# A retention and gated-FFN kernel: q of the first 512 tokens in 1-KB pieces, and tables made by one multiply each

## The chip, the cores and the metric

The kernel runs on one core of a Trainium2 chip. The metric is the device time of one execution in microseconds (us). A core has a matmul engine (TensorE, "PE" in the profile, with its weight loads as "PEld"), VectorE ("DVE"), ScalarE ("ACT"), GpSimd ("POOL"), SyncE ("SP", which here issues transfers), and 16 DMA engines that move data between HBM and the on-chip memory SBUF. PE writes its results to PSUM, eight banks of 2 KB a partition; PE, DVE and ACT are ordered among each other by semaphores, and each works through its own instructions in order.

## The reference

```python
# q, k, v: (8, 8, 576, 64) float32; x: (4608, 512); w_gate, w_val: (512, 1536); w_out: (1536, 512)
scores = scale * np.matmul(q, k.transpose(0, 1, 3, 2))
gamma = 1.0 - 2.0 ** (-5.0 - np.arange(H, dtype=np.float32))
rel = pos[:, None] - pos[None, :]
Dmat = np.where(rel >= 0, gamma[:, None, None] ** rel[None, :, :], 0.0)
ret = scores * Dmat[None, :, :, :]
attn = np.matmul(ret, v)
x = attn.transpose(0, 2, 1, 3).reshape(B * S, H * D)
gate = 1.0 / (1.0 + np.exp(-(x @ w_gate)))
out = (gate * (x @ w_val)) @ w_out
```

Eight batches of eight heads go through a causal attention without softmax whose scores decay by a factor per head and distance; its output, 4,608 tokens by 512, goes through a gated feed-forward layer.

## The kernel before

The decay gamma^(i-j) is split: q is multiplied by gamma^i (and the scale), k by gamma^-j, from small tables, while both are cast from float32 to bf16. What remains of the decay is the causal mask, multiplied into the scores on their way out of PSUM. Tokens are worked in chunks of 128; what earlier chunks contribute comes through a state (k transposed times v, summed over tokens, `st`), so that a chunk needs only its own scores (`intra`) and one product of q with the state before it (`inter`).

The first 768 tokens are worked as three pairs of chunks, `PAIRS`: pair 0 and pair 1 are tokens 0 to 255 and 256 to 511 of batch 0, pair 2 is the first 256 tokens of batch 1. The rest runs later, in steps of one chunk, beside the feed-forward matmuls of finished tokens.

A pair A is loaded by `load_pair` in six transfers of 256 KB on SP: k, q, k, q, v, v, each of four heads (half g = 0 or 1), two neighbouring tokens a partition, so that a contiguous piece is 2 tokens x 64 x 4 B = 512 B. Pairs 0 and 1 are issued first: k and q of both halves of pair 0, then of pair 1, then the four transfers of v, then the weights of the feed-forward layer. All of them use one pool of 18 buffers, `ld`.

Each half is then worked as follows. `cast_pair` multiplies by the table and casts (k on POOL, q on DVE; v is cast alone, on POOL). `turn` calls `pair_t`: four PE transposes of 128 x 128 put two heads by 64 dimensions on the partitions, into one PSUM bank, and ACT copies that bank to SBUF. k keeps its two token parities apart (`kT`), while q is written into token order (`qT`), that is to every second element. `pair_qk` makes the scores of a half in 16 small matmuls into two banks, and DVE multiplies them by the mask `trip` into `ptp`. Then follow `pair_intra`, `pair_st` (the state matmuls), `tile_sv` (ACT copies the state to `sbd`), `pair_inter` and `pair_out` (a copy to `xT`, the input of the feed-forward layer).

The order of the instructions of each engine is written out by hand: the statements at the end of the function give it, one after the other, and each engine takes its own in that order. The groups of matmuls called `fill(n)`, 4n of them on a blank tile into a bank that nobody reads, stand between the first steps. The turned k of a half goes through the bank of pool `tr` and the turned q through that of `pv` (one buffer each); the last q turn uses a bank of pool `ffn`. `pv` and `tr` later hold the outputs of pair 0.

The tables are made by `tables`: an iota of token positions on POOL, for each head one multiply by log(gamma) on DVE, and an exponential each for k and q on ACT. It is called for the pairs (positions 2p + r in each of two 256-token blocks) and for the single chunks.

The start of the order, as written:

```python
    cast_pair("q", 0, 0, nc.vector)
    turn("k", 0, 0, *TR)
    turn("q", 0, 0, *PV)
    fill(3)
    cast_pair("q", 0, 1, nc.vector)
    pair_qk(0, 0, QK)
    turn("k", 0, 1, *TR)
    fill(2)
    turn("q", 0, 1, *PV)
    fill(3)
```

Of the kernel before, what the change touches and what calls it, by code (L numbers as in the profile page):

```python
# [9 lines left out]
FP32 = mybir.dt.float32  # L10
BF16 = mybir.dt.bfloat16
AF = mybir.ActivationFunctionType
ALU = mybir.AluOpType
# [3 lines left out]
def kernel(  # L17
# [30 lines left out]
    consts = ctx.enter_context(tc.tile_pool(name="consts", bufs=1))  # L48
    ld_pool = ctx.enter_context(tc.tile_pool(name="ld", bufs=18))
# [4 lines left out]
    osb_pool = ctx.enter_context(tc.tile_pool(name="osb", bufs=13))  # L54
# [12 lines left out]
    PAIRS = [(0, 0), (0, 1), (1, 0)]  # L67
# [28 lines left out]
    parts = {}  # L96
# [9 lines left out]
            tiles.append(t)  # L106
        loaded[s] = tiles

    def load_pair(A):

        b, a2 = PAIRS[A]
        for nm, src, g in (("k", k, 0), ("q", q, 0), ("k", k, 1), ("q", q, 1), ("v", v, 0), ("v", v, 1)):
            t = ld_pool.tile([P, M, 2, D], FP32, tag="ld", name=f"{nm}32p_{A}_{g}")
            nc.sync.dma_start(  # L114
                out=t.rearrange("p h r d -> p h (r d)"),
                in_=src[b, g * M:(g + 1) * M, a2 * 2 * P:(a2 + 1) * 2 * P, :].rearrange("h (p r) d -> p h (r d)", r=2))
            parts[nm, "pair", A, g] = t
            yield

    def load_w(f, nf):  # L120

        for nm, src in (("g", moe_w_gate), ("v", moe_w_val)):
            for i in range(nf):
                r = NKC // nf
                t = ld_pool.tile([P, r, nf * P], FP32, tag="ld", name=f"w{nm}32_{f}_{i}")
                nc.sync.dma_start(
                    out=t, in_=src[i * r * P:(i + 1) * r * P, f * P:(f + nf) * P].rearrange("(c p) f -> p c f", p=P))
                parts[nm, f, i] = t

    def load_wo(f):  # L130
        t = ld_pool.tile([P, DM], FP32, tag="ld", name=f"wo32_{f}")
        nc.sync.dma_start(out=t, in_=moe_w_out[f * P:(f + 1) * P, :])
        parts["o", f] = t

    both = [load_pair(A) for A in range(2)]
    for n_pair in (4, 2):
        for one in both:
            for _ in range(n_pair):
                next(one)
    load_w(0, 2)  # L140
    load_w(2, 2)
    load_w(4, 4)
    load_w(8, 4)
    pair_2 = load_pair(2)
    for n_wo, n_pair in ((2, 4), (6, 2), (4, 0)):
        for _ in range(n_wo):
            load_wo(sum(1 for x in parts if x[0] == "o"))
        for _ in range(n_pair):
            next(pair_2)
    LEAD_CAST = 3  # L150


# [5 lines left out]
    def idle_bank():  # L158
        idle.append(ffn_psum.tile([P, P], FP32, tag="ffn", name=f"idle_{len(idle)}"))
# [9 lines left out]
    def tables(shape, pattern, step, put):  # L169

        pos = consts.tile([P, pattern[0][1], pattern[1][1]], FP32, name=f"pos{step}")
        nc.gpsimd.iota(pos, pattern=pattern, base=0, channel_multiplier=step,
                       allow_small_or_imprecise_dtypes=True)
        arg = consts.tile(shape, FP32, name=f"arg{step}")
        qt = consts.tile(shape, FP32, name=f"qtab{step}")
        kt = consts.tile(shape, FP32, name=f"ktab{step}")
        for h in range(H):
            nc.vector.tensor_scalar_mul(put(arg, h), pos, math.log(1.0 - 2.0 ** (-5.0 - h)))
        nc.scalar.activation(out=kt, in_=arg, func=AF.Exp, bias=0.0, scale=-1.0)
        nc.scalar.activation(out=qt, in_=arg, func=AF.Exp, bias=lnscale, scale=1.0)  # L180
        return qt, kt

    lnscale = consts.tile([P, 1], FP32)
    nc.vector.memset(lnscale, math.log(1.0 / math.sqrt(D)))
    qtab2, ktab2 = tables([P, 2, H, 2], [[2 * P, 2], [1, 2]], 2, lambda t, h: t[:, :, h, :])
    ident = consts.tile([P, P], BF16)
    make_identity(nc, ident)
    qtab, ktab = tables([P, NC, H, 1], [[P, NC], [1, 1]], 1, lambda t, h: t[:, :, h, :])
# [46 lines left out]
    natural = {}  # L235
    turned = {}

    def cast_pair(nm, A, g, eng):

        if (nm, A) not in natural:  # L240
            natural[nm, A] = osb_pool.tile([P, 2, H, D], BF16, tag="osb", name=f"{nm}p_{A}")
        o = natural[nm, A][:, :, g * M:(g + 1) * M, :].rearrange("p r h d -> p h r d")
        i = parts.pop((nm, "pair", A, g))
        if nm == "v":
            eng(out=o, in_=i)
        else:
            tab = (ktab2 if nm == "k" else qtab2)[:, PAIRS[A][1], g * M:(g + 1) * M, :].unsqueeze(3).to_broadcast([P, M, 2, D])
            eng.tensor_tensor(out=o, in0=i, in1=tab, op=ALU.mult)

    def cast_k(s):  # L250

        b, c = STEPS[s]
        n = width[c]
        k32 = loaded[s][0]
        kn = qk_nat[s % NB][:, 1:3]
        for j in range(n // 64):
            for hh in range(2):
                nc.gpsimd.tensor_tensor(  # L258
                    out=kn[half(hh), j, :, half(hh)], in0=k32[half(j), hh::2, :],
                    in1=ktab[half(j), c, hh::2].unsqueeze(2).to_broadcast([64, M, D]), op=ALU.mult)  # L260
        natural["k", s] = kn
# [38 lines left out]
    turned = {}  # L300
# [6 lines left out]
    def half(x):  # L307
        return slice(x * 64, x * 64 + 64)
# [3 lines left out]
    def pair_t(nm, A, g, psum, tag, eng):  # L312
        ps = psum.tile([P, 2, 2, P], BF16, tag=tag, name=f"{nm}Tp_{A}_{g}")
        for i in range(2):
            for r in range(2):
                m = 2 * g + i
                nc.tensor.matmul(ps[:, i, r, :], lhsT=natural[nm, A][:, r, 2 * m:2 * m + 2, :], rhs=ident,
                                 is_transpose=True, start=(i == 0 and r == 0), stop=(i == 1 and r == 1))
        if nm == "k":
            if g == 0:  # L320
                turned["kp", A] = osb_pool.tile([P, M, 2, P], BF16, tag="osb", name=f"kT_{A}")
            o = turned["kp", A][:, 2 * g:2 * g + 2]
        else:
# [3 lines left out]
        eng(out=o, in_=ps)  # L327
# [45 lines left out]
    def pair_intra(A, g, a):  # L373
        s = 2 * A + a
        if s not in pair_ps:
            pair_tile(A, a, [(tr_psum, "tr") if a else (pv_psum, "pv")])
        for i in range(2):
            m = 2 * g + i
            ps, at_m, of = pair_ps[s][m]
            for r in range(2):  # L380
                for hh in range(2):
                    nc.tensor.matmul(ps[half(hh), at_m, :], lhsT=natural["v", A][half(a), r, 2 * m + hh, :],
                                     rhs=probs["p", A][half(a), hh, m, r, :],
                                     start=(at_m == 0 and r == 0), stop=(at_m == of - 1 and r == 1),
                                     skip_group_check=True)
# [224 lines left out]
    def turn(nm, A, g, pool=ffn_psum, tag="ffn"):  # L610
        pair_t(nm, A, g, pool, tag, on_act)
# [23 lines left out]
    for A in range(2):  # L635
        for g in range(2):
            cast_pair("k", A, g, nc.gpsimd)
# [7 lines left out]
    QK = [(qk_psum, "qk"), (qk_psum, "qk")]  # L645
    FF = [(ffn_psum, "ffn"), (ffn_psum, "ffn")]
    TR, PV = (tr_psum, "tr"), (pv_psum, "pv")
    cast_pair("q", 0, 0, nc.vector)
    turn("k", 0, 0, *TR)
    turn("q", 0, 0, *PV)  # L650
    fill(3)
    cast_pair("q", 0, 1, nc.vector)
    pair_qk(0, 0, QK)
    turn("k", 0, 1, *TR)
    fill(2)
    turn("q", 0, 1, *PV)
# [12 lines left out]
    fill(3)  # L669
    pair_intra(0, 0, 0)  # L670
    pair_qk(1, 1, FF)
    pair_intra(0, 0, 1)
# [205 lines left out]
```

## Time and profile before

| | before |
|---|---|
| median of 9 runs | 335.19 us (335.04 to 335.61) |
| the profiled execution, whole | 335.19 us |
| its span in the profile | 333.5 us |
| weight loads of PE (PEld) busy | 190.3 us, 57% |
| HBM read, written | 37.75 MB, 9.44 MB |
| packets of the main DMA queue | 163,920 |

The span runs from the first to the last profiled instruction; some 1.7 us of the whole time lie around it. Busy times overlap between engines. In a row of the timeline the first number is the start in us from the span's start, the second the length, then come engine, line, operation, what is written from what, and in square brackets how long the engine had been idle before and what ended that idle time. L248 is the cast of q or k in `cast_pair`, L327 the copy in `pair_t`, L336 the scores, L341 the mask, L382 `pair_intra`, L351 `pair_st`, L362 `tile_sv`, L400 `pair_out`, L245 the cast of v. A matmul's shape is given as rows x columns of its weights and then of what streams through.

The loads of the first pairs, in the page's part on DMA issues (KB each, median us from issue to landing):

```profile
k32p<-in_k_dram SPq DMA_DIRECT2D x6, 256.0 KB, 5.0
q32p<-in_q_dram SPq DMA_DIRECT2D x6, 256.0 KB, 5.2
v32p<-in_v_dram SPq DMA_DIRECT2D x6, 256.0 KB, 6.0
```

### The profile page before, as it was taken

The numbers are of one execution on the slowest core, as the hardware profiler recorded it, in microseconds if no ns is written. First come the engines' busy times: TensorE is split into PE (matmuls) and PEld (weight loads), VectorE is DVE, ScalarE is ACT, GpSimd is POOL, SyncE is SP. The second block draws the span as 40 slices with busy tenths as digits, with TensorE's granted clock in tenths as the row PEclk, the third lists the DMA queues.
The fourth block names the chain that finished last, engine by engine and source line by source line (L and its number), as shares of the span: only waits on it lengthen the run. The fifth ranks groups of instructions, "written<-read, shape, count | busy, mean of one in ns | idle before, by whom it ended". The sixth has DMA issues, their size and how long they took to land.

```text
span 333.5 us, 7568 instructions
## 1 busy us (share of the span) xinstructions
PE 326.9 (98%) x2868; PEld 190.3 (57%) x2868; DVE 168.5 (51%) x337; ACT 167.5 (50%) x345; POOL 183.5 (55%) x322
## 2 busy tenths in 40 slices
PE   8899999999999999999999999999999999999996
PEld 7764546869566566566566555544555455444443
DVE  6847749726476166345247636442674256504320
ACT  6554636547466365355456554445546455233321
POOL 5588558788979977572458966572677400000000
PEclk9999999999999999999999999999999999999999
DMA  8999999999999999999756999599765950020002
GB/s 222 316 373 361 322 243 174 203 183 210 191 232 185 191 225 187 275 198 248 146 104 139 203 222 192 115 209 264 136 129 81 272 188 0 2 95 31 2 31 94
DMA packets 164100, 60.00 MB, mean 180 GB/s; under 512 B 144480, under 2 KB 156000, under 8 KB 164064
## 3 DMA queue, kind: packets, MB, share of 16 engines
q1 hardware_dynamic: 163920, 59.39, 84.6%
q8 instruction: 22, 0.36, 0.5%
q10 hardware_dynamic: 144, 0.13, 0.1%
q14 instruction: 14, 0.11, 0.1%
HBM read 37.75 MB, written 9.44 MB: 141 GB/s over the span
## 4 chain that ended last, share of the span: by engine, by line
PE 89%; DMA 4%; DVE 2%; SPq 2%; issue 1%; ACT 1%; POOL 0%; DVEq 0%
PE h L506 49%; PE op L572 24%; PE hg L621 3%; PE hv L621 3%; DMA q<-in_q_dram 2%; PE pv L431 2%; PE qk L410 2%; DMA v32p<-in_v_dram 2%; PE pv L429 2%; PE st L443 2%; SPq L114 2%; PE op L562 1%; DVE vbd L279 1%; PE hg L700 1%; PE hv L700 1%
## 5 line engine op out<-in xcount | busy, mean ns | idle before, releaser
L506 PE MATMUL h<-xT,wg_sb 128*128 128x384 bf16 (+2 forms) x480 | 102.8, 337 | 0.3 <-DVE gv L534 0.2
L506 PE MATMUL h<-xT,wv_sb 128*128 128x384 bf16 (+2 forms) x480 | 102.8, 337 | 0.0
L258 POOL TENSOR_TENSOR qk_nat<-k,ktab 64x256 bf16<-64x256 f32 x120 | 73.8, 615 | 43.2 <-PE st L443 30.2
L534 DVE TENSOR_TENSOR gv<-g,h 128x384 bf16<-128x384 bf16 (+1 forms) x96 | 59.7, 621 | 71.8 <-PE h L506 56.3
L572 PE MATMUL op<-wo_sb,gv 128*128 128x512 bf16 x372 | 85.5, 379 | 0.0
L530 ACT ACTIVATE g<-h 128x384 bf16<-128x384 f32 (+1 forms) x96 | 52.2, 544 | 64.9 <-PE h L506 58.3
L449 DVE CAST sbd<-st 64x256 bf16<-64x256 f32 x104 | 43.7, 420 | 45.1 <-PE st L443 42.9
L506 PEld LDWEIGHTS <-wg_sb 128*128 128x128 bf16 x480 | 43.6, 98 | 31.8 <-DVE ob L549 0.6
L506 PEld LDWEIGHTS <-wv_sb 128*128 128x128 bf16 x480 | 44.1, 98 | 29.0 <-issue 0.4
L279 POOL CAST vbd<-v 64x256 bf16<-64x256 f32 x116 | 46.4, 400 | 16.4 <-PE pv L431 11.9
L572 PEld LDWEIGHTS <-gv 128*128 128x128 bf16 x372 | 34.3, 98 | 36.3
L289 ACT CAST vs<-v 64x256 bf16<-64x256 f32 x104 | 41.9, 403 | 2.4 <-DMA v<-in_v_dram 0.8
L549 ACT COPY ob<-op 128x512 f32<-128x512 f32 x33 | 19.3, 586 | 46.2 <-PE op L572 44.9
L268 POOL TENSOR_TENSOR qk_nat<-q,qtab 128x512 bf16<-128x512 f32 (+1 forms) x32 | 33.3, 1042 | 2.6 <-POOL qk_nat L258 0.2
L433 ACT CAST xT<-pv 128x512 bf16<-128x512 f32 (+1 forms) x34 | 18.2, 534 | 18.1 <-PE pv L431 18.0
L412 DVE TENSOR_TENSOR pt<-qk,tri 128x512 bf16<-128x512 f32 (+1 forms) x34 | 21.2, 625 | 6.1 <-PE qk L410 5.8
L443 PEld LDWEIGHTS <-qk_nat 128*128 128x128 bf16 x208 | 13.2, 98 | 8.7
L431 PE MATMUL pv<-pt,vbd 128*128 128x64 bf16 x240 | 18.0, 193 | 0.0
L431 PEld LDWEIGHTS <-vbd 128*128 128x128 bf16 x240 | 15.2, 98 | 3.5
L429 PE MATMUL pv<-T,sbd 128*128 128x64 bf16 x216 | 17.2, 193 | 0.0
L429 PEld LDWEIGHTS <-sbd 128*128 128x128 bf16 x216 | 15.1, 98 | 2.5
L522 DVE TENSOR_TENSOR gv<-g,h 128x256 bf16<-128x256 bf16 x24 | 10.0, 420 | 11.9 <-ACT g L520 11.4
(84 smaller groups left out, 242.8 us busy)
## 6 DMA issues: line engine op xcount, KB each, us to landing
out_dram<-ob SPq DMA_DIRECT2D x34, 256.0 KB, 2.9
k<-in_k_dram SPq DMA_DIRECT2D x26, 256.0 KB, 3.9
q<-in_q_dram SPq DMA_DIRECT2D x26, 256.0 KB, 4.6
v<-in_v_dram SPq DMA_DIRECT2D x26, 256.0 KB, 5.3
wg<-in_moe_w_gate_dram SPq DMA_DIRECT2D x12, 256.0 KB, 6.1
wv<-in_moe_w_val_dram SPq DMA_DIRECT2D x12, 256.0 KB, 5.4
wo<-in_moe_w_out_dram SPq DMA_DIRECT2D x12, 256.0 KB, 5.3
k32p<-in_k_dram SPq DMA_DIRECT2D x6, 256.0 KB, 5.0
```

Source lines behind the costliest of these rows:

```text
L258: nc.gpsimd.tensor_tensor(out=kn[half(hh), j, :, half(hh)], in0=k32[half(j), hh::2, :], in1=ktab[half(j), c, hh::2].unsqueeze(2).to_broadc ...
L268: eng.tensor_tensor(out=qs[0:n], in0=q32[0:n], in1=qtab[0:n, c, :].unsqueeze(2).to_broadcast([n, H, D]), op=ALU.mult)
L279: eng(out=vb[half(hh), j, :, half(hh)], in_=v32[half(j), hh::2, :])
L289: nc.scalar.copy(out=natural["vs", s][half(hh), j], in_=loaded[s][2][half(j), hh::2, :])
L412: nc.vector.tensor_tensor(out=pt[:, :, 0:n].rearrange("p m (j t) -> p m j t", t=64), in0=qkp[:, :, 0:n].rearrange("p m (j t) -> p m j t", ...
L429: nc.tensor.matmul(pvp[:, m, half(j)], lhsT=before[:, m, :], rhs=qT[:, m, half(j)], start=True, stop=False)
L431: nc.tensor.matmul(pvp[:, m, half(j)], lhsT=vb[:, j, m, :], rhs=pt[:, m, half(j)], start=before is None, stop=True)
L449: nc.vector.tensor_copy(out=sb[half(hh), :, half(hh)], in_=st_tiles[b][half(hh)])
L506: nc.tensor.matmul(out, lhsT=w_sb[:, kc, fc * P:(fc + 1) * P], rhs=xT[:, kc, t0 + a:t0 + e], start=(kc == 0), stop=(kc == NKC - 1))
L530: nc.scalar.activation(out=g[:, 0:n], in_=h1[:, 0:n], func=AF.Sigmoid)
L534: nc.vector.tensor_tensor(out=gvs[some[0]][:, a:e], in0=g[:, 0:n], in1=h2[:, 0:n], op=ALU.mult)
L572: nc.tensor.matmul(opp, lhsT=gvs[fc][:, nb * P:(nb + 1) * P], rhs=wo_sb[:, fc, :], start=(fc == 0), stop=(fc == NFC - 1))
```

## The change

q of pairs 0 and 1 (tokens 0 to 511 of batch 0) is no longer loaded by pair. Four transfers `load_quads(m)` of the same 256 KB each take two heads and all 512 tokens, four neighbouring tokens a partition, so that a contiguous piece is 1 KB. Partition p then holds tokens 4p to 4p + 3, so partitions 0 to 63 belong to pair 0 and 64 to 127 to pair 1. `cast_quads` multiplies and casts one such tile on DVE with a table of its own (`qtab4`); `turn_quads` transposes it in four PE instructions; two tiles (four heads, m even and odd) share the PSUM bank of pool `pv`; and `take_quads(A, g)` copies on ACT the columns of one pair out of that bank into `qT`, to every fourth element. There are as many casts, transposes and copies of q as before, but each copy takes half of the columns of two transposed tiles, and the bank is free only when both pairs' copies are done.

The order of the loads becomes k, q, q, k, q, q, then k twice, then v; the order of the first steps is rewritten, with 15 groups of fillers after the first ten instead of 14, all casts of q ahead of the first mask on DVE, and no second idle bank. k, v and the whole of pair 2 are loaded and worked as before.

The tables are made with one multiply by a tile of eight log(gamma) values, set by eight memsets, in place of eight multiplies by a constant; a third call makes `qtab4`.

```diff
-    both = [load_pair(A) for A in range(2)]
-    for n_pair in (4, 2):
-        for one in both:
-            for _ in range(n_pair):
-                next(one)
+    def load_quads(m):
+
+        t = ld_pool.tile([P, 2, 4, D], FP32, tag="ld", name=f"q32q_{m}")
+        nc.sync.dma_start(out=t.rearrange("p h r d -> p h (r d)"),
+                          in_=q[0, 2 * m:2 * m + 2, 0:4 * P, :].rearrange("h (p r) d -> p h (r d)", r=4))
+        parts["q", "quads", m] = t
+
+    for g in range(2):
+        load_part("k", 0, g)
+        for i in range(2):
+            load_quads(2 * g + i)
+    for g in range(2):
+        load_part("k", 1, g)
+    for A in range(2):
+        for g in range(2):
+            load_part("v", A, g)
...
-        for h in range(H):
-            nc.vector.tensor_scalar_mul(put(arg, h), pos, math.log(1.0 - 2.0 ** (-5.0 - h)))
...
+    decay = consts.tile([P, H], FP32)
+    for h in range(H):
+        nc.vector.memset(decay[:, h:h + 1], math.log(1.0 - 2.0 ** (-5.0 - h)))
...
+        nc.vector.tensor_tensor(out=arg, in0=pos.unsqueeze(2).to_broadcast([P, n, H, r]),
+                                in1=decay.unsqueeze(1).unsqueeze(3).to_broadcast([P, n, H, r]), op=ALU.mult)
...
+    ktab2, qtab2 = tables(2, 2, 2 * P, 2, "kq")
+    qtab4, = tables(1, 4, 0, 4, "q")
...
+    def cast_quads(m):
+        if m % 2 == 0:
+            natural["quads", m // 2] = osb_pool.tile([P, 2, 4, 2, D], BF16, tag="osb", name=f"qq_{m // 2}")
+        o = natural["quads", m // 2][:, m % 2].rearrange("p r h d -> p h r d")
+        tab = qtab4[:, 0, 2 * m:2 * m + 2, :].unsqueeze(3).to_broadcast([P, 2, 4, D])
+        nc.vector.tensor_tensor(out=o, in0=parts.pop(("q", "quads", m)), in1=tab, op=ALU.mult)
+
+    quads = {}
+
+    def turn_quads(m, psum, tag):
+        if m % 2 == 0:
+            quads[m // 2] = psum.tile([P, 2, 4, P], BF16, tag=tag, name=f"qTq_{m // 2}")
+        for r in range(4):
+            nc.tensor.matmul(quads[m // 2][:, m % 2, r, :], lhsT=natural["quads", m // 2][:, m % 2, r, :, :], rhs=ident,
+                             is_transpose=True, start=(m % 2 == 0 and r == 0), stop=(m % 2 == 1 and r == 3))
+
+    def take_quads(A, g):
+        if ("qp", A) not in turned:
+            turned["qp", A] = osb_pool.tile([P, M, 2 * P], BF16, tag="osb", name=f"qT_{A}")
+        nc.scalar.copy(out=turned["qp", A][:, 2 * g:2 * g + 2, :].rearrange("p m (t r) -> p m r t", r=4),
+                       in_=quads[g][:, :, :, half(A)])
...
-    cast_pair("q", 0, 0, nc.vector)
+    for m in range(2):
+        cast_quads(m)
     turn("k", 0, 0, *TR)
-    turn("q", 0, 0, *PV)
+    turn_quads(0, *PV)
+    fill(2)
+    turn_quads(1, *PV)
+    take_quads(0, 0)
     fill(3)
-    cast_pair("q", 0, 1, nc.vector)
+    for m in range(2, 4):
+        cast_quads(m)
     pair_qk(0, 0, QK)
     turn("k", 0, 1, *TR)
+    take_quads(1, 0)
     fill(2)
-    turn("q", 0, 1, *PV)
+    turn_quads(2, *PV)
+    turn_quads(3, *PV)
+    take_quads(0, 1)
     fill(3)
-    cast_pair("q", 1, 0, nc.vector)
+    turn("k", 1, 0, *TR)
     pair_qk(0, 1, FF)
-    turn("k", 1, 0, *TR)
-    turn("q", 1, 0, *PV)
-    fill(2)
-    cast_pair("q", 1, 1, nc.vector)
+    take_quads(1, 1)
+    fill(3)
     turn("k", 1, 1, *TR)
     pair_qk(1, 0, QK)
-    fill(1)
-    turn("q", 1, 1)
-    idle_bank()
-    fill(3)
+    fill(2)
     pair_intra(0, 0, 0)
     pair_qk(1, 1, FF)
```

More of the change, by code (lines that the diff above doesn't have):

```diff
@@ L107, in load @@
         loaded[s] = tiles
[L109 to L118, printed above, removed]
     def load_w(f, nf):
@@ L133, in load_wo, with load_part @@
         parts["o", f] = t
-    both = [load_pair(A) for A in range(2)]
-    for n_pair in (4, 2):
-        for one in both:
-            for _ in range(n_pair):
-                next(one)
+    def load_part(nm, A, g):
+        b, a2 = PAIRS[A]
+        t = ld_pool.tile([P, M, 2, D], FP32, tag="ld", name=f"{nm}32p_{A}_{g}")
+        nc.sync.dma_start(
+            out=t.rearrange("p h r d -> p h (r d)"),
+            in_={"k": k, "q": q, "v": v}[nm][b, g * M:(g + 1) * M, a2 * 2 * P:(a2 + 1) * 2 * P, :].rearrange(
+                "h (p r) d -> p h (r d)", r=2))
+        parts[nm, "pair", A, g] = t
+    def load_quads(m):
[12 more added lines that the diff above has]
+            load_part("v", A, g)
     load_w(0, 2)
@@ L143 @@
     load_w(8, 4)
-    pair_2 = load_pair(2)
+    pair_2 = iter((("k", 0), ("q", 0), ("k", 1), ("q", 1), ("v", 0), ("v", 1)))
     for n_wo, n_pair in ((2, 4), (6, 2), (4, 0)):
@@ L148 @@
         for _ in range(n_pair):
-            next(pair_2)
+            nm, g = next(pair_2)
+            load_part(nm, 2, g)
     LEAD_CAST = 3
@@ L168, with tables @@
     fill(10)
[L169 to L176, printed above, removed]
-        for h in range(H):
-            nc.vector.tensor_scalar_mul(put(arg, h), pos, math.log(1.0 - 2.0 ** (-5.0 - h)))
-        nc.scalar.activation(out=kt, in_=arg, func=AF.Exp, bias=0.0, scale=-1.0)
-        nc.scalar.activation(out=qt, in_=arg, func=AF.Exp, bias=lnscale, scale=1.0)
-        return qt, kt
     lnscale = consts.tile([P, 1], FP32)
     nc.vector.memset(lnscale, math.log(1.0 / math.sqrt(D)))
-    qtab2, ktab2 = tables([P, 2, H, 2], [[2 * P, 2], [1, 2]], 2, lambda t, h: t[:, :, h, :])
+    decay = consts.tile([P, H], FP32)
+    for h in range(H):
+        nc.vector.memset(decay[:, h:h + 1], math.log(1.0 - 2.0 ** (-5.0 - h)))
+    def tables(n, r, base, step, which):
+        pos = consts.tile([P, n, r], FP32, name=f"pos{step}")
+        nc.gpsimd.iota(pos, pattern=[[base, n], [1, r]], base=0, channel_multiplier=step,
+                       allow_small_or_imprecise_dtypes=True)
+        arg = consts.tile([P, n, H, r], FP32, name=f"arg{step}")
+        nc.vector.tensor_tensor(out=arg, in0=pos.unsqueeze(2).to_broadcast([P, n, H, r]),
+                                in1=decay.unsqueeze(1).unsqueeze(3).to_broadcast([P, n, H, r]), op=ALU.mult)
+        made = []
+        for nm in which:
+            t = consts.tile([P, n, H, r], FP32, name=f"{nm}tab{step}")
+            if nm == "k":
+                nc.scalar.activation(out=t, in_=arg, func=AF.Exp, bias=0.0, scale=-1.0)
+            else:
+                nc.scalar.activation(out=t, in_=arg, func=AF.Exp, bias=lnscale, scale=1.0)
+            made.append(t)
+        return made
+    ktab2, qtab2 = tables(2, 2, 2 * P, 2, "kq")
+    qtab4, = tables(1, 4, 0, 4, "q")
     ident = consts.tile([P, P], BF16)
     make_identity(nc, ident)
-    qtab, ktab = tables([P, NC, H, 1], [[P, NC], [1, 1]], 1, lambda t, h: t[:, :, h, :])
+    ktab, qtab = tables(NC, 1, P, 1, "kq")
     qtab = qtab.rearrange("p c h o -> p c (h o)")
```

## The prediction

> **What bounds the kernel now.** I read the page first (shares, chain of waits), then the chain in order of time up to 45 us, then the timeline of the first 20 us with the windows of that stretch, and last the timeline around 50 us.
>
> The page's busy shares, one row of five engines:
>
> ```profile
> PE 326.9 (98%) x2868; PEld 190.3 (57%) x2868; DVE 168.5 (51%) x337; ACT 167.5 (50%) x345; POOL 183.5 (55%) x322
> ```
>
> TensorE (PE) is busy nearly the whole span of 333.5 us; what an edit at the start can win or lose is how early PE's dense stream begins. The chain in order of time (start, length, what) says what set that:
>
> ```profile
> 6.52 6.47 DMA v32p<-in_v_dram
> 12.99 0.05 issue
> 13.04 0.63 POOL vp L245
> 13.67 0.04 issue
> 13.71 0.39 PE st L351 x12
> ```
>
> The start is bound by the tenth load, the second half of v of pair 0: it lands at 12.99, GpSimd (POOL) casts it, and PE's state matmuls (`pair_st(0, 0)`) end at 14.10. From there the chain is PE and the short ACT copies of the state. So transfers set the start, and q's four of 256 KB each lie before v in the queue. The windows (width, PE, PEld, DVE, ACT, POOL, granted clock, DMA share, GB/s) show the queue saturated, at two rates:
>
> ```profile
> 11.00:12.00 1.00, 1.00 (x30) 0.91 (x29) 0.83 (x2) 0.61 (x2) 0.61 (x1) 1.00 1.20 294
> 15.00:16.00 1.00, 1.00 (x42) 0.86 (x43) 0.39 (x2) 0.60 (x2) 0.85 (x2) 1.00 1.09 348
> ```
>
> At 11 us the pieces are 512 B (q, k, v of a pair); at 15 us mostly the first weights, in 1-KB pieces. 256 KB take 262/294 = 0.89 us in the first and 262/348 = 0.75 us in the second.
>
> How close behind the transfers the engines are is seen in the timeline of the first 15 us:
>
> ```profile
> 4.58 0.81 DVE L248 TENSOR_TENSOR qp<-q32p,qtab 128x512 bf16<-128x512 f32 x1 [0.55 <-DMA q32p<-in_q_dram]
> 5.88 0.73 ACT L327 COPY qT<-qTp 128x512 bf16<-128x512 bf16 x1
> 6.67 0.42 PE L336 MATMUL qkp<-qT,kT 64*64 64x128 bf16 x16 [0.15 <-ACT qT L327]
> 8.91 0.42 PE L336 MATMUL qkp<-qT,kT 64*64 64x128 bf16 x16 [0.15 <-ACT qT L327]
> 12.54 0.41 PE L382 MATMUL pvp<-ptp,vp 64*64 64x128 bf16 x8
> 13.71 0.38 PE L351 MATMUL st<-vp,kp 64*64 64x64 bf16 x12 [0.30 <-POOL vp L245]
> 14.92 0.44 PE L351 MATMUL st<-vp,kp 64*64 64x64 bf16 x16 [0.58 <-ACT sbd L362]
> ```
>
> PE waited only 0.30 us for the cast of v. That is the whole slack between the q/k path and the transfers: if the path becomes later by more than about half a microsecond, it sets the start in v's place.
>
> Far later one more place matters: near 50 us VectorE (DVE) waits a little for a transfer before a chain of DVE work that holds PE up:
>
> ```profile
> 49.29 1.09 DVE L268 TENSOR_TENSOR qk_nat<-q,qtab 128x512 bf16<-128x512 f32 x1 [0.17 <-DMA q<-in_q_dram]
> ...
> 53.83 0.61 PE L506 MATMUL h<-xT,wg_sb 128*128 128x256 bf16 x4
> ```
>
> **What the Trainium skill says.** "DMA: Bandwidth & Descriptors", section "Why small descriptors are slow (HBM only)", gives each packet a fixed overhead of about 3 cycles beside one cycle for 32 B: 19 cycles for 512 B, 35 for 1 KB, so 1 KB should be 8% faster. The trace agrees in sign and shows more, 348 against 294 GB/s (18%). "SBUF — State Buffer", section "Door 1: The DMA port swizzle (why `[64,N]` ≈ `[32,N]`)", speaks of 16-byte lines and says that two-byte elements may be strided up to 8 apart for free. The trace differs: ScalarE (ACT) pays for a stride of 2:
>
> ```profile
> L327 ACT COPY kT<-kTp x6: 580/586/586, 5.3 to 39.5; 128x512 bf16<-128x512 bf16 x6
> L327 ACT COPY qT<-qTp x6: 735/739/742, 5.9 to 40.2; 128x512 bf16<-128x512 bf16 x6
> ```
>
> Same size, contiguous 586 ns, every second element 739 ns. The new copy writes every fourth element; no row shows one.
>
> **The change part by part.**
>
> Tables: 16 multiplies of about 0.1 us (1.59 us together) become 8 memsets and 3 multiplies, one ACT row more (about 0.14 us at ACT's spacing) and one iota more on POOL (about 0.2 us). The first cast of k waits for its transfer until 3.80 with POOL idle 0.85 us before it, ACT is free until 5.34, DVE waits for q until 4.58 with 0.55 idle. All hidden, value 0. Without that cover it would be 0.2 us late on POOL.
>
> Transfers: same 256 KB each, same number, on SP before the same things. The four q transfers go from 0.89 to 0.75 us: v lands 4 x 0.14 = 0.56 us earlier, at about 12.4, and its cast ends at 13.1. Bounds: 0.3 us (the page's 8%) to 0.6. This would be the gain if v still ended last.
>
> Order: q of pairs 0 and 1 is now held in tiles of two heads by 512 tokens. The first score block of pair 0 needs two such tiles (second and third transfer) instead of one. Step by step, with PE at about 0.055 us a filler or turn (the timeline has 12 fillers in 0.83 and four turns in 0.40: 0.43 for eight more, so 0.23 for four and 0.17 to drain), 0.35 for 16 score matmuls (6.67 to the next start at 7.02), hand-over 0.05:
> - tile 0: cast on DVE 4.43 to 5.2 (4.58 less 0.15); tile 1: the third landing was 1.33 after the second (POOL starts 5.91 against 4.58), less 0.14: cast 5.6 to 6.3. Four turns on PE 6.35 to 6.6, drained 6.77. ACT copy 6.8 to 7.55. Scores (0,0) at 7.6, before 6.67: 0.9 late.
> - turn of k (0,1) at 7.95 (its cast ends near 7.5). ACT: k copy 8.4 to 9.0, then q's copy for pair 1 to 9.65. Tiles 2 and 3 are turned into the same PSUM bank, so they wait for that copy: PE 9.7 to 10.15, with fill(2) before it and about 1 us idle. Queued behind are the turns and scores of everything later. ACT copies to 11.1; scores (0,1) at 11.15, before 8.91: 2.2 late.
> - From there the new order is shorter: two q turns and their waits before scores (1,0) are gone. fill(3), turn of k (1,1), scores (1,0) at 12.45 (before 10.97), fill(2), `pair_intra(0,0,0)` at 13.25 (before 12.54), scores (1,1), `pair_intra(0,0,1)`, state matmuls from 14.1 to 14.6 (before 14.10). Late by 0.5.
> - DVE: its q casts are all before the first mask, so masks run 8.75 to 10.0, 11.7 to 13.0, 13.0 to 14.3 and 14.3 to 15.6 (four pairs of 1.29; before the last ended at 14.51). The copy of the first output tile then ends at 16.3 instead of 15.11, and frees the bank for `pair_intra(1,0,0)`: PE there at 16.35 instead of 15.62. Late by 0.7. Unknown: 0.5 if DVE catches up.
>
> Fillers: 24 groups of four become 25, 0.23 us; contained in the steps above. The second idle bank goes; no instruction.
>
> Later: weights land 0.56 earlier, and the casts of them are not what PE waits for there. From 17 to 48 us PE is dense, so the shift is carried. At 49.29 the 0.17 us wait for q's transfer takes up that much of it. Loads of pair 2 and the later steps are unchanged.
>
> Sum: 0.7 - 0.17 = about +0.5 us. The profiled execution is 335.19 us, 1.7 over its span, and equals the median: forecast 335.7. Own range 335.3 to 336.1: the third landing 0.4 earlier takes 0.4 off until k's cast binds, three ACT copies in series on the path at +0.1 each add 0.3.
>
> **Rivals.**
> - Faster: v keeps ending last. Then the whole 0.56 arrives: 334.6. For it: slack existed, the tail of the old q turns disappears, and one late transfer less would pull the first steps in. Against: two transfers before the first scores and the shared bank. Needs the path to be 0.8 us quicker than my steps.
> - Slower: ACT's stride-4 copy. Place: three of the four copies (first of tile pair 0, pair 1's from the same bank, first of tile pair 1) are in series with PE. Price: stride 2 cost 0.153 us over contiguous; if stride 4 costs two to three times that, 0.89 to 1.05 us each, the path is 0.45 to 0.9 us later, 336.2 to 336.6; taken at 0.95: 335.7 + 3 x 0.21 = 336.3. It decides from about 0.80 us a copy on (3 x 0.06 brings 335.86).
> - No difference: the 0.5 is absorbed by the ACT and DVE waits after 14 us (0.58 us in the row at 14.92) and at 50 us: 335.2. Against: those waits are on state copies that move along with PE.
>
> **How the numbers follow.** A measurement of this kernel can tell 0.2%, 0.67 us: faster is below 334.52, slower above 335.86. Chances: forecast 0.44, slow copies 0.31, v still last 0.16, absorbed 0.09. Slower: all of the slow copies and 0.4 of the forecast's, 0.31 + 0.18 = 0.49. Faster: three quarters of v still last, 0.12. Same: 0.39. The range 334.6 to 336.7 leaves out half of the fast case (0.08) and the top of the slow one (0.1).
>
> **What would show it.** Right: scores (0,0) near 7.6 and (0,1) near 11.2; a PE gap of about 1 us before the turns of tiles 2 and 3 ended by ACT; v's cast near 12.5 with nobody waiting for it; state matmuls ending at 14.4 to 14.8; ACT copies of q near 0.74 us. Wrong: PE again waiting for v's cast (the fast case), copies over 0.8 us (the slow one), q transfers still 0.89 us apart (the pieces bring nothing), or a PE shift at 20 us that is gone by 60 us for another reason.

## The result and the profile after

| | before | after |
|---|---|---|
| median | 335.22 us, 31 runs (334.49 to 338.15) | 337.68 us, 10 runs (336.98 to 338.30) |
| ratio, 95% interval | | 1.0068 (1.0052 to 1.0085) |
| profiled execution, its span | 335.19, 333.5 us | 336.98, 335.3 us |

The change costs about 2.3 us by the ratio (0.68% of 335.2); forecast were +0.5 us and a range up to 336.7. Some executions of most versions run with a lowered clock for a few microseconds near the start and take 1 to 4 us more; they are in the medians and in the ratios alike, and "at full clock" below means a median without them (for after 337.31, 2.1 us above before).

TensorE's busy time, in the page's busy shares, did not change (326.9 us before), nor did the share:

```profile
PE 327.0 (98%) x2872; PEld 191.3 (57%) x2872; DVE 169.2 (50%) x332; ACT 169.6 (51%) x346; POOL 184.8 (55%) x323
```

So the 1.8 us by which the span grew are time in which PE stood still, at the start. The timeline of after (start, length, engine, line, what; in brackets the idle time before and what ended it) shows where. L275 is the cast of q, L283 its transposes, L289 the copy of q on ACT, L378 the scores, L424 `pair_intra`, L442 the copy `xT`:

```profile
6.11 0.69 DVE L275 TENSOR_TENSOR qq<-q32q,qtab 128x512 bf16<-128x512 f32 x1 [0.67 <-DMA q32q<-in_q_dram]
...
7.30 1.30 ACT L289 COPY qT<-qTq 128x512 bf16<-128x512 bf16 x1 [0.75 <-PE qTq L283]
8.65 0.42 PE L378 MATMUL qkp<-qT,kT 64*64 64x128 bf16 x16 [0.72 <-ACT qT L289]
9.91 1.30 ACT L289 COPY qT<-qTq 128x512 bf16<-128x512 bf16 x1
11.27 0.61 PE L283 MATMUL qTq<-ident,qq 128*128 128x128 bf16 x8 [1.43 <-ACT qT L289]
11.91 1.31 ACT L289 COPY qT<-qTq 128x512 bf16<-128x512 bf16 x1 [0.69 <-PE qTq L283]
13.27 0.42 PE L378 MATMUL qkp<-qT,kT 64*64 64x128 bf16 x16 [0.50 <-ACT qT L289]
...
17.48 1.28 DVE L442 CAST xT<-pvp 128x512 bf16<-128x512 f32 x2
18.21 0.63 PE L424 MATMUL pvp<-ptp,vp 64*64 64x128 bf16 x24 [0.19 <-POOL wv_sb L245]
```

Three times in this stretch PE stands still until a copy of q ends on ACT, and each copy takes 1.30 us, not the 0.74 of before. All four are alike, as the view of the tile `qT` says (min, median and max in ns):

```profile
L289 ACT COPY qT<-qTq x4: 1300/1304/1309, 7.3 to 13.5; 128x512 bf16<-128x512 bf16 x4
```

v is no longer waited for by PE. In the timeline of POOL its first two casts run one after the other without a wait, and those that wait now serve steps that are not due yet:

```profile
11.71 1.29 POOL L265 CAST vp<-v32p 128x512 bf16<-128x512 f32 x2
13.27 0.62 POOL L265 CAST vp<-v32p 128x512 bf16<-128x512 f32 x1 [0.28 <-DMA v32p<-in_v_dram]
```

The second half of v of pair 0 landed at 12.33, before at 12.99, close to the 12.4 of the forecast, but this is in part luck. The first half landed at 11.46, before at 11.22: up to there nothing was gained, since the third transfer landed 1.67 us behind the second, before 1.36. Then before had a pause: its second half of v came 1.77 us behind the first, where 0.9 is usual. In after a pause (1.31) falls two transfers later. Past both pauses 0.25 us are left, as the cast of the last half of v shows, which waits for its transfer in both (after, then before):

```profile
14.58 0.62 POOL L265 CAST vp<-v32p 128x512 bf16<-128x512 f32 x1 [0.69 <-DMA v32p<-in_v_dram]
```

```profile
14.83 0.62 POOL L245 CAST vp<-v32p 128x512 bf16<-128x512 f32 x1 [0.25 <-DMA v32p<-in_v_dram]
```

The place of such pauses changes from one execution to another: in e11 below, which is the kernel before once more, the fourth transfer comes 1.94 us behind the third. Their cause is not known. What was gained nobody could use.

The chain of waits, which went through v's load before, now leaves the transfers of q, k and v out:

```profile
11.47 6.08 DMA wv<-in_moe_w_val_dram
17.55 0.05 issue
17.61 0.63 POOL wv_sb L245
18.23 0.61 PE pvp L424 x23
```

This is to be read with care. `pair_intra` does not use the weights; it needs the PSUM bank that the copy `xT` frees. The first of the two copies in the row at 17.48 takes 0.68 us and ends at 18.16, some 0.06 us before POOL's cast, so the chain took the one that came last; PE begins at 18.21. In two other versions with the same order (e3 and e5 below) the same row names DVE's copy.

Later, part of the delay is made up. The first `h` matmul of the stretch near 50 us is 1.79 us late (55.62 against 53.83), the first `hg` was 2.47 late (19.70 against 17.23). DVE's wait of 0.17 us for a transfer of q is gone from its row:

```profile
51.10 0.67 DVE L310 TENSOR_TENSOR qk_nat<-q,qtab 128x512 bf16<-128x512 f32 x1
...
55.62 0.60 PE L548 MATMUL h<-xT,wg_sb 128*128 128x256 bf16 x4
```

From there to the end the distance stays at 1.8 us.

### The profile page after: what moved, and what is told of

It reads as the page before. It is cut to its first block, busy times and chain, and to the rows that moved or that the text cites. A ratio compares the mean times of both kernels' runs of the same rounds, so it can differ in the third digit from the quotient of the medians.

```text
span 335.3 us, 7576 instructions
## 1 busy us (share of the span) xinstructions
PE 327.0 (98%) x2872; PEld 191.3 (57%) x2872; DVE 169.2 (50%) x332; ACT 169.6 (51%) x346; POOL 184.8 (55%) x323
## 4 chain that ended last, share of the span: by engine, by line
PE 92%; SPq 3%; DMA 2%; issue 1%; DVE 1%; ACT 0%; POOL 0%
PE h L548 49%; PE op L614 24%; PE op L837 3%; PE hv L663 3%; PE hg L663 3%; PE pv L473 2%; PE qk L452 2%; PE pv L471 2%; SPq L128 2%; DMA wv<-in_moe_w_val_dram 2%; PE st L485 2%; PE op L604 1%; SPq L137 1%; PE pvp L424 1%; PE hv L745 1%
## 5 line engine op out<-in xcount | busy, mean ns | idle before, releaser
L321 POOL CAST vbd<-v 64x256 bf16<-64x256 f32 x116 | 46.0, 397 | 16.4 <-PE pv L473 11.9
```

The source lines that it names most:

```text
L321: eng(out=vb[half(hh), j, :, half(hh)], in_=v32[half(j), hh::2, :])
```

## The experiments

The theory: the ACT copy, whose write goes to every fourth element, is slow, three copies are in series with PE, and that is the loss. Its rivals: the copy is slow because of what it reads (runs of 64 columns out of PSUM); the shared bank and the wait for two tiles are the loss; the tables or the transfers matter after all. Ratios are to runs of the kernel before on the same chip, with the 95% interval; losses and gains at full clock are against the same runs.

**e1: the copy written contiguously, read as in after.** The columns of q stay grouped by token modulo 4, and the matmuls that stream q pick every 64th element (128 bytes).

```diff
-        nc.scalar.copy(out=turned["qp", A][:, 2 * g:2 * g + 2, :].rearrange("p m (t r) -> p m r t", r=4),
+        nc.scalar.copy(out=turned["qp", A][:, 2 * g:2 * g + 2, :].rearrange("p m (r t) -> p m r t", r=4),
...
+        return q_t.rearrange("p (r t) -> p t r", r=4)[:, a * 32:(a + 1) * 32, :]
```

> The changed kernel with its q copies written contiguously (q grouped by token remainder; the matmuls pick the columns in token order by a strided read). Theory (the ACT copies that write every fourth element, 1.30 us instead of the 0.74 I took, make the start late): copies at about 0.6 us, three of them in series on PE's path, so 3 x 0.7 = about 2.1 us less than the changed kernel: 335.2 to 335.6. Rival 1 (the order and the shared bank make it late): the copies shorten but PE still waits, at most 0.7 us less: 336.8. Rival 2 (the cost is in reading 64-column runs out of PSUM, not in writing): the copies stay near 1.3 us and the time at 337.5.

Measured: 342.29 us, ratio 1.0196 (1.0167 to 1.0226): a miss in time, an answer on the copy. From the views of the two tiles:

```profile
L289 ACT COPY qT<-qTq x4: 585/588/592, 7.8 to 13.0; 128x512 bf16<-128x512 bf16 x4
...
L384 PE MATMUL qkp<-qT,kT x64: 372/392/393, 8.4 to 16.8; 64*64 64x128 bf16 x64
```

The copy reads the same runs out of PSUM and takes 588 ns, as much as the wholly contiguous copies of k (586): reading is not what costs, that rival falls. But PE pays for reading q at 128-byte steps: 392 ns a score matmul instead of 216, and 16 of them take 1.05 us instead of 0.42. Moreover the clock that PE was granted was at half of the full one for a while afterwards, as the windows show (width, five engines, clock, DMA share, GB/s):

```profile
22.00:24.00 2.00, 2.00 (x11) 1.27 (x11) 0.63 (x2) 0.58 (x2) 1.70 (x5) 0.50 1.01 347
24.00:26.00 2.00, 2.00 (x24) 1.28 (x23) 0.00 (x0) 1.29 (x4) 1.96 (x3) 0.50 1.02 375
26.00:28.00 2.00, 2.00 (x11) 1.45 (x10) 0.42 (x1) 0.10 (x1) 2.00 (x4) 0.50 1.03 371
```

So its time says little of the copy alone.

**e2: tiles 2 and 3 turned into a bank of their own.** This takes the wait for the shared bank away and leaves the copy as it is.

```diff
-    turn_quads(2, *PV)
-    turn_quads(3, *PV)
+    turn_quads(2, st_psum, "st")
+    turn_quads(3, st_psum, "st")
```

> The changed kernel with q tiles 2 and 3 turned into a bank of their own (that of the state, not yet in use). Theory (slow copies in series on ACT): the turns of tiles 2 and 3 no longer wait for pair 1's copy, but their own copy still queues behind it on ACT, so scores (0,1) come about 0.7 us earlier: 336.8. Rival (the shared bank is the cause): the gap of 1.4 us before these turns goes and the whole loss with it: 335.2 to 335.6.

Measured: 336.66 us, ratio 1.0021 (1.0008 to 1.0035). At full clock it loses 1.2 us, after 2.1: about 0.9 us goes. The turns run at 10.10 without a wait, and what is late next is again the copy; in the timeline:

```profile
10.33 2.46 ACT L289 COPY qT<-qTq 128x512 bf16<-128x512 bf16 x2
12.85 0.42 PE L378 MATMUL qkp<-qT,kT 64*64 64x128 bf16 x16 [1.24 <-ACT qT L289]
```

The scores of the second half start only 0.42 us earlier than in after (13.27), because the copies for pair 1 and pair 0 run one behind the other on ACT. (The first scores were 0.42 us later than in after, at 9.07, so from there on e2 is 0.84 quicker.)

**e3: everything of after but the 1-KB pieces.** Each tile is loaded in two transfers, one for each pair, with two tokens a partition (512-B pieces), so that the copies write every second element; the table for q is copied together from that of the pairs.

```diff
-        nc.sync.dma_start(out=t.rearrange("p h r d -> p h (r d)"),
-                          in_=q[0, 2 * m:2 * m + 2, 0:4 * P, :].rearrange("h (p r) d -> p h (r d)", r=4))
+        for b in range(2):
+            nc.sync.dma_start(out=t[:, :, 2 * b:2 * b + 2].rearrange("p h r d -> p h (r d)"),
+                              in_=q[0, 2 * m:2 * m + 2, 2 * b * P:2 * (b + 1) * P, :].rearrange("h (p r) d -> p h (r d)", r=2))
...
-        nc.scalar.copy(out=turned["qp", A][:, 2 * g:2 * g + 2, :].rearrange("p m (t r) -> p m r t", r=4),
-                       in_=quads[g][:, :, :, half(A)])
+        nc.scalar.copy(out=turned["qp", A][:, 2 * g:2 * g + 2, :].rearrange("p m (t r) -> p m r t", r=2),
+                       in_=quads[g][:, :, 2 * A:2 * A + 2, :])
```

> The new order and two heads a tile, but in 512-B pieces: two tokens a partition for each pair, so that q is copied to every second element again as before. Eight q transfers of 128 KB instead of four of 256 KB. Theory: copies back at 0.74 us; with transfers 0.3 us later at the second tile and v at its old time, scores (0,1) about 1.4 us earlier than in the changed kernel, time 336.0 (335.7 to 336.3). Rival (order alone costs the loss): 337.5 or more.

Measured: 335.45 us, ratio 0.9990 (0.9976 to 1.0004): no difference from before, with the new order, two heads a tile and the shared bank. Its copies in the view of the tile, and its scores of the two halves of pair 0 in the timeline:

```profile
L292 ACT COPY qT<-qTq x4: 733/736/750, 7.5 to 12.5; 128x512 bf16<-128x512 bf16 x4
```

```profile
8.24 0.42 PE L381 MATMUL qkp<-qT,kT 64*64 64x128 bf16 x16 [0.15 <-ACT qT L292]
11.88 0.42 PE L381 MATMUL qkp<-qT,kT 64*64 64x128 bf16 x16
```

The first scores are 0.41 us earlier than in after, the second 1.39: two more copies lie between, each 0.57 shorter. e8 gave this version a separate bank and e6's order: 335.51 us, ratio 1.0000 (0.9981 to 1.0019), nothing more to win.

> 512-B pieces and stride-2 copies in the new order, with tiles 2 and 3 in a bank of their own and their copy for pair 0 first, one fill(3) fewer. Theory: the late start of the new order at stride 2 (state matmuls about 0.8 us later than in the kernel before) shrinks to 0.3 us or less: 334.9 to 335.4. Rival (bank without weight): as e3, 335.4 to 335.6.

**e4: the stride put into the kernel before.** Loads, order and banks of before; only the copies of pairs 0 and 1 write every fourth element. q's columns of these pairs are then in another token order, so the output is not the reference's; the work is the same.

```diff
-            o = turned["qp", A][:, 2 * g:2 * g + 2, :].rearrange("p m (t r) -> p m r t", r=2)
+            o = turned["qp", A][:, 2 * g:2 * g + 2, :].rearrange("p m (t r) -> p m r t", r=2 if A == 2 else 4)
+            if A < 2:
+                ps = ps.rearrange("p m a (b t) -> p m (a b) t", b=2)
```

> The kernel before, with only the q copies of pairs 0 and 1 written to every fourth element out of a contiguous PSUM bank; q's columns are then in another token order, so the scores are of other tokens than the reference's. Theory (stride of the writes): the four copies take about 1.3 us instead of 0.74; each of the first three stands directly between a turn and the scores, +0.56 each, against about 0.3 us of slack: 336.3 to 336.9. Rival (reading 64-column runs is what costs): copies stay at 0.74 us, time 335.2.

Measured: 336.78 us, ratio 1.0033 (1.0018 to 1.0048), a loss of 1.3 us at full clock, with the copies at 1306 ns out of one contiguous bank (view of the tile) and PE waiting for three of them by 0.7 to 0.8 us each (timeline):

```profile
L329 ACT COPY qT<-qTp x4: 1305/1306/1310, 6.1 to 13.9; 128x512 bf16<-128x512 bf16 x4
```

```profile
7.46 0.42 PE L338 MATMUL qkp<-qT,kT 64*64 64x128 bf16 x16 [0.83 <-ACT qT L329]
10.27 0.42 PE L338 MATMUL qkp<-qT,kT 64*64 64x128 bf16 x16 [0.72 <-ACT qT L329]
12.90 0.42 PE L338 MATMUL qkp<-qT,kT 64*64 64x128 bf16 x16 [0.82 <-ACT qT L329]
```

So the write stride alone makes the copy slow and the kernel slower. In the old order it costs 1.3 us, in the new one with its shared bank 2.1, of which e2 took off 0.9.

**e5: 1-KB pieces with a contiguous write.** As in e1 the columns stay grouped by token modulo 4, but PE streams them in runs of 32 as they lie; the mask of these pairs is made in the same order, and the rows are put in order by the store of the output.

```diff
-                                         rhs=turned["qp", A][half(hh), m, a * P:(a + 1) * P], start=True, stop=True)
+                                         rhs=q_cols(A, half(hh), m, a), start=True, stop=True)
...
+        return q_t.rearrange("p (r t) -> p r t", r=4)[:, :, a * 32:(a + 1) * 32]
...
+        if r < 4 * P:
+            nc.sync.dma_start(out[r:r + P, :].rearrange("(t r) d -> r t d", r=4), ob)
+            return
```

> The changed kernel with contiguous q copies and matmuls that read q in runs of 32 columns: the columns of the first 512 tokens stay grouped by remainder through scores, mask and output, and the output rows are put in order by the store. 1-KB pieces, two heads a tile and the shared bank stay. Theory (the stride of ACT's writes is the loss): copies 0.59 us, three in series save 3 x 0.71 = 2.1 us, PE's clock stays full: 335.2 to 335.7 where the kernel before has 335.4. Rival (something else of the new order): 336.5 or more.

Measured: 335.41 us, ratio 0.9998 (0.9988 to 1.0009). The whole loss is gone, with the pieces, the order and the bank of after. In the view of the tile both sides of the hand-over are at their old price:

```profile
L391 PE MATMUL qkp<-qT,kT x64: 213/216/240, 8.3 to 14.3; 64*64 64x128 bf16 x64
...
L296 ACT COPY qT<-qTq x4: 586/589/593, 7.7 to 12.2; 128x512 bf16<-128x512 bf16 x4
```

e6 added e2's bank, moved `take_quads(0, 1)` ahead of `take_quads(1, 0)` and left out one `fill(3)`: 335.10 us, ratio 0.9981 (0.9961 to 1.0000), at the edge of what can be told from no change. With short copies the shared bank is worth little.

> As the run before it, with tiles 2 and 3 in a bank of their own, their copy for pair 0 ahead of the copies for pair 1, and one group of fillers (fill(3)) fewer. Theory: with short copies the bank is what is left of the loss; scores (0,1) near 10.6 us instead of about 11.2, state matmuls end near 14.1: 334.8 to 335.3. Rival (the bank does not matter once the copies are short): the same as the run before it.

**e7 and e9: the new tables alone, in the kernel before.** Two series of the same kernel; its edit is the part of the change that concerns `tables`, without `qtab4`.

> The kernel before with the new way of making the tables only. Both theories: it is hidden under the first transfers, 335.2 to 335.5, no difference that can be measured. A cost at the very start (first turn of k later than 4.9 to 5.3 us by the tables) would show as 0.2 us or more.

> The kernel before with the new tables, once more and in more rounds, since the first look gave 334.6 against 335.4 where nothing was expected. If the tables are worth something by themselves: again 0.4 to 0.9 us below the kernel before, and its timeline shows the state matmuls of pair 0 ending before 14.1 us. If that was chance: within 0.3 us of the kernel before.

Measured: 334.60 and 334.58 us, ratios 0.9953 (0.9932 to 0.9974) and 0.9962 (0.9943 to 0.9981). A gain of 0.7 to 0.9 us at full clock where none was expected. The kernel before against itself (e11) gave 0.9985 (0.9964 to 1.0006), so two series of one kernel can lie 0.15% apart by the ratio (0.15 us by the medians at full clock); this gain is two to three times that, and came twice.

> The kernel before against itself: a second profile of it, and what two equal kernels differ by in such a comparison. Ratio 1.000 within 0.002; if it differs as much as the run with the tables alone did (0.995), that result says nothing.

After with the old eight multiplies for each table (e10) ran at 337.33 us, ratio 1.0037 (1.0021 to 1.0054); at full clock it loses 1.8 us, after 2.1. The 0.3 between them is not much beside the 0.16 by which the kernel before differs from chip to chip (335.31 to 335.47 at full clock), and it points the other way: there the edit of the tables shows no gain.

> The changed kernel with its tables made by eight multiplies each again (24 multiplies with the third table), all else as changed. If the tables matter only at the very start and PE then waits for ACT's copies anyway: 337.3 to 337.7, as the changed kernel. If the new tables are worth 0.7 us inside the changed kernel too: about 338.1.

What e7 and e9 change besides the arithmetic is the size of the constants, and so where the load buffers `ld` begin in SBUF. The compiled kernels place them, per partition, at byte 117,984 before (224 over a multiple of 256), at 118,016 in e7 and e9 (a multiple of 256), at 118,304 in after (32 over) and at 118,272 in e10 (a multiple of 256). In the window of e9 from 9 to 10 us the same 512-B transfers run at 349 GB/s, before at 305. e12, e13 and e14 test this without touching what is computed: a small constant tile is made larger, which moves the buffers behind it.

```diff
-    warm = consts.tile([P, 1], FP32)
-    nc.scalar.activation(out=warm, in_=lnscale, func=AF.Sigmoid)
+    warm = consts.tile([P, 16], FP32)
+    nc.scalar.activation(out=warm[:, 0:1], in_=lnscale, func=AF.Sigmoid)
```

In e12 (16 columns) the kernel before has its buffers at a multiple of 256; in e13 (48 columns) at 128 over; e14 is e9 with 64 columns, and so again at 224 over.

> The kernel before, tables and all, with one constant tile made 60 bytes longer, which moves the load buffers by 32 bytes a partition, to multiples of 256 bytes. If the place of the buffers is what the tables changed: 512-B transfers 0.75 us apart and 334.5 to 334.9. If the tables' own work is: 0.90 us apart and 335.3 to 335.7.

> The same with 188 bytes more, load buffers at multiples of 128 bytes but not of 256. If 256 is what counts: 0.90 us apart, 335.3 to 335.7. If any multiple of 64 or 128 will do: as the run before it.

> The new tables in the kernel before, with the load buffers moved back to the remainder that they had before (224 bytes over a multiple of 256). If place counts: 0.90 us apart and 335.3 to 335.7, the gain of the tables gone. If the tables' work counts: 334.6 again.

| run | tables | load buffers, over a multiple of 256 B | median us | ratio (95%) |
|---|---|---|---|---|
| e12 | old | 0 | 334.67 | 0.9969 (0.9956 to 0.9982) |
| e13 | old | 128 | 335.41 | 0.9998 (0.9976 to 1.0020) |
| e9 | new | 0 | 334.58 | 0.9962 (0.9943 to 0.9981) |
| e14 | new | 224 | 335.23 | 0.9989 (0.9960 to 1.0018) |

The gain goes with the place of the buffers and not with the tables. The earlier experiments owe nothing to it: their buffers lie 32 over (e2, e5, e6), 128 over (e3, e8) and 224 over (e4). (The larger constant moves every buffer behind it; that it is the load buffers that count is read from the transfers.) The windows from 9 to 10 us, in this order of kernels (e12, e13, e9, e14), have it in their last column:

```profile
9.00:10.00 1.00, 0.85 (x25) 0.68 (x23) 0.72 (x3) 0.43 (x1) 0.72 (x1) 1.00 1.20 359
```

```profile
9.00:10.00 1.00, 0.84 (x25) 0.78 (x25) 0.98 (x3) 0.17 (x2) 0.24 (x2) 1.00 1.20 289
```

```profile
9.00:10.00 1.00, 0.85 (x25) 0.79 (x25) 0.94 (x3) 0.17 (x2) 0.75 (x1) 1.00 1.17 349
```

```profile
9.00:10.00 1.00, 0.84 (x25) 0.69 (x23) 0.85 (x2) 0.27 (x1) 0.23 (x2) 1.00 1.20 286
```

The DMA engines are as busy in all four (the column before, 1.17 to 1.20); in aligned buffers, those that begin at a multiple of 256 bytes, they move 21 to 26% more. POOL's casts of k show the same without a window: k is every second transfer, and in e9 two of its casts start 1.49 us apart, before 1.81.

```profile
7.76 1.04 POOL L256 TENSOR_TENSOR kp<-k32p,ktab 128x512 bf16<-128x512 f32 x1 [0.51 <-DMA k32p<-in_k_dram]
9.25 1.25 POOL L256 TENSOR_TENSOR kp<-k32p,ktab 128x512 bf16<-128x512 f32 x1 [0.44 <-DMA k32p<-in_k_dram]
```

The gain does not come where v is awaited: `pair_intra(1,0,0)` begins at 15.73 in e12, at 15.62 in before, although v's second half landed 0.67 us earlier (12.32); e12's third transfer landed later, which held q and k back. In these two traces the gain comes at two places further on, at which before waits for transfers. Behind the first, near 20 us, where POOL waits for a weight and PE stands still, e12 is 0.38 us ahead; behind the second, near 50 us, where DVE waits for q, 0.66.

**e15: the best of both.** e6 with its load buffers at a multiple of 256 (`warm` with 64 columns).

> 1-KB pieces, contiguous q copies with the columns kept in groups, tiles 2 and 3 in a bank of their own, and load buffers at multiples of 256 bytes. If place counts, the loads of k and v come 0.15 us each earlier than in the run without the shift: 334.0 to 334.8, level with or below the kernel before with the tables alone. If PE's own order is the limit by now: 335.1 as without the shift.

Measured: 334.70 us, ratio 0.9973 (0.9958 to 0.9987): faster than before and after, and no better than e12 on the same chip (334.67), which is the kernel before with one constant made larger. In aligned buffers the 1-KB pieces and the new order add nothing to the time.

## Why the prediction was wrong

It named the right sign as likeliest (0.49 for slower) and the mechanism as its slower rival, and was too low by 2 us in the number; even the rival's end, 336.6, and the range's, 336.7, were too low.

**The step that failed** is the price of the ACT copy. The forecast took 0.74 us, the rival "if stride 4 costs two to three times that, 0.89 to 1.05 us each". It measured 1.30: over the contiguous copy (0.59) stride 2 costs 0.15 and stride 4 0.72, nearly five times as much, not two or three. The bound was drawn through one point. The count of three copies in series was right: 3 x 0.56 = 1.68 us of delay that the forecast did not have. e4 shows that the stride alone does it, e5 that without it nothing is lost.

**The second term** is the landing of the third transfer. Tile 1's cast was put at 5.6 and began at 6.11, 0.5 late; the first scores at 7.6 became 8.65, which is 0.5 of landing and 0.56 of copy. The forecast took the distance from the second landing to the third from one trace, where it is 1.36 us (1.33 between the casts). In the seven other traces with the loads of before it is 1.36 (e4) to 1.87 (e12), and over 1.5 in all but e4; in after it is 1.67. So the delay does not belong to the new loads; what sets the distance was not found. e3 and e5 have the delay as well and lose nothing, so alone it costs no time.

Put together on the forecast's own steps: scores (0,1) at 11.15 became 13.27, by 0.5 + 3 x 0.56 = 2.2; the state matmuls' end at 14.6 became 16.4, since the stretch between took 3.13 us and not 3.45. From there the forecast carried a further delay by DVE to `pair_intra(1,0,0)`, at 16.35; it was 18.21, 1.86 later, the same error carried on. At that point after is 2.59 us behind before; 0.12 of it goes in the next steps, 0.41 near 20 us and 0.27 near 50, and 1.79 remain, where 0.5 was forecast. So the profiled execution lies 1.28 us above the forecast; it is the quickest of the ten, the median lies higher.

**Right, by its steps:** v is no longer waited for; tiles 2 and 3 wait for the shared bank, with a PE gap of about 1 us ended by ACT (1.43); DVE's wait near 50 us takes up part of the delay (0.17 forecast; 0.27 measured across that stretch). Not forecast were the 0.41 us near 20 us of before, where the prediction called PE dense: there before's PE stands still for 0.25 us while a weight that landed 1.49 us behind the one before it is cast, and after, 2 us later, does not. Right in the number and not in the way was v's landing: of the 0.66 us that it came earlier 0.25 outlast the pauses, and the first weights come 0.24 earlier (15.30 against 15.54), not 0.56. Two of the four q transfers took the less time that was forecast (0.74 instead of 0.84 behind the one before, 0.75 instead of 0.90), the last did not (0.94), and the second is the late third landing.

**The rival "v keeps ending last"** fell: the q path sets the start. Even in before it was close: e12, where v came 0.67 us earlier and the third transfer 0.34 later, starts no earlier. The prediction called 0.30 us the whole slack of this path and then reckoned with half a microsecond; with 2 us of delay that decided nothing. "No difference" would have been right for a copy at stride 2 or 1, as e3 and e5 show. That e3 loses nothing also suggests that the forecast's +0.5, with copies at 0.74, was too high by about that much: in e3 `h` near 54 us is 0.4 us late in the trace, but the median of 20 runs does not show it.

**The tables** were put at 0. For the arithmetic that holds (e14). What the prediction did not see is that their edit moves the load buffers, which is worth 0.7 us in the kernel before (e12) and shows little where ACT's copies set the start (e10 has its buffers at a multiple of 256 and still loses 1.8 us). Its step on the transfers needs an addition by the same route. The 0.89 against 0.75 us for 256 KB was read from buffers at one place, 224 bytes over a multiple of 256, and there it is the size of the pieces. In aligned buffers both are quicker: 512-B pieces land 0.75 us apart and the first weights, in 1-KB pieces, about 0.67 (e12). So the piece is worth some 17% of the time in the one place and 11% in the other, where it is nearer to the prediction's estimate of 8%; and the place is worth as much as the piece.

## What to carry to other kernels

A change of layout has to be priced with the copy that undoes it: look for the step with which that copy writes, measure that very step instead of extending a neighbouring one, and if it is slow, keep the columns grouped and put them in order at the store. Before loads are rearranged for longer pieces, look at where their buffers begin; moving them to a multiple of 256 bytes brought more here than the whole rearrangement. An edit that seems to touch arithmetic alone can move every buffer allocated after it, so a small gain from it should be tested against a mere shift.

## What the runs showed of the hardware

- ScalarE's copy of 128x512 bf16 from PSUM to SBUF takes 588 ns when it writes contiguously, 736 to every second element and 1304 to every fourth (e1, e3, e4 and after). Reading runs of 64 columns out of PSUM costs nothing that shows (588 against 586 for a contiguous copy).
- TensorE streaming bf16 at 128-byte steps took 392 ns a matmul of 128 columns instead of 216; in runs of 32 columns 216. In that version the granted clock was 0.50 from about 21.5 to 28.4 us, though PE was busy from 20 us on. That the slow matmuls caused this was not tested.
- In a full queue, loads of 256 KB in 512-B pieces land 0.75 us apart in buffers that begin at a multiple of 256 bytes, and 0.90 at 32, 128 and 224 bytes over one (after, e13, before); other remainders were not tried. In 1-KB pieces it is about 0.67 (e12) and 0.75 (before, after). The Trainium skill, "DMA: Bandwidth & Descriptors", section "How a descriptor splits into AXI transactions", says that the first transaction of a descriptor that does not start at a multiple of 256 bytes begins at the multiple below it, so that bytes are fetched without use, and speaks of reading. Here the source is the same in all runs and the destination in SBUF decides; whether the same splitting is behind it, no run shows.
